# A searched table that assigns small operations to engines, Silu in five front chunks, and newly searched instruction orders, in a Conformer block on one core

## The chip, the cores and the metric

The kernel runs on one core of a Trainium2 chip. Its time is what the device needs for one execution, in microseconds (us). Engines are named as the profiler names them: PE multiplies matrices (PEld loads its weights), ACT evaluates functions, DVE and POOL do element-wise work, SP issues transfers.

## The reference

One Conformer block on x of shape (2, 4000, 144) in bf16, with four heads of width 36:

```python
h = _layernorm(x); x = x + 0.5 * (_silu(h @ w_ff1a) @ w_ff1b)          # 144 -> 576 -> 144
h = _layernorm(x); q, k, v = split heads of h @ w_qkv
p = _softmax(q @ k^T * Dh ** -0.5)                                     # 4000 x 4000, per batch and head
x = x + (p @ v) @ w_o
h = _layernorm(x) @ w_pw1; a, b = halves of h
h = a * _sigmoid(b)
c = depthwise convolution of h over time, 5 taps
x = x + _silu(c) @ w_pw2
h = _layernorm(x); x = x + 0.5 * (_silu(h @ w_ff2a) @ w_ff2b)
return _layernorm(x)
```

The largest part is attention: for each of 2 batches and 4 heads 4000 x 4000 scores, their exponentials, and the sums over values.

## The kernel before

**Tiling.** The 8000 tokens are cut into 16 chunks of 500 (`CH`), eight to a batch; a chunk is four blocks of 125 tokens. For each chunk the kernel runs the first feed-forward, the projections to Q, K and V, attention, the output projection, the gated convolution, and the second feed-forward. Attention of one chunk goes over 62 key tiles of 64 keys (`KT_ROWS`) and a rest of 32. One tile holds the scores of all four heads (PE, four quarter-array matmuls `PS<-QT,KT`), their exponentials (`PT<-PS`) and the sums (`PS<-PT,VA`). There are 1008 tiles in all, written in the constant `TYPES` by a letter each. An "A" tile takes its exponential on ACT, as one instruction over 128 x 1000. A "D" tile takes it on DVE in five instructions (two conversions `PT<-PS` of 128 x 500 to an integer form, two bit operations and one product `PT<-PT` of 128 x 1000); it leaves two factors, so that PE needs eight sum matmuls in place of four. "R" is the rest tile of a chunk.

**How the order comes about.** The Python code first runs a planner. Coroutines (one for each step of each chunk: `ln`, `ff`, `residual`, `proj`, `glu`, `conv`, `epilogue` and so on) ask for an engine and buffers, and a cost model picks which goes next. Every operation is noted with what it reads and writes (`R.op`). The instructions are issued by one helper line, so that all have the same line in the profile (L546 before, L580 after), and tiles tell them apart. The planner's result is then replaced: `settle` builds the attention tiles anew from `TYPES`, `BANKS` and `SLOTS`, and `arrange` sorts each engine's instructions into the order written out in the constant `ORDER`; the waits follow from the dependencies.

```python
lines[e] = [o for i in at for o in blocks[keys[i]]]
```

Here `at` is the decoded string of `ORDER` for engine `e`. So the order on every engine is fixed at build time, and a wait blocks all that stands behind it on that engine.

**Three stages.** In the front only little attention can run: keys and values come chunk by chunk. `silus` counts the front's Silu activations; only when none is left does one table load on ACT change to the exponential's table, and no exponential goes before it. Before the change only chunk 0 uses Silu in the front (six activations); the other chunks take `tanh` on ACT (`TH<-PS`) and form x * (1 + tanh) by one DVE product (`HT<-TH,PS`). In the middle, exponentials run back to back while feed-forwards, projections and convolutions of other chunks fill the other engines. Behind the last exponential lies the tail (`mode["tail"]`): output projection, convolution and second feed-forward of the last chunks, with Silu again.

**Where small operations run.** A LayerNorm (`ln`) is a statistics instruction on DVE (`ST<-X`), one scaling (`RS<-ST`), one power on POOL (`RS<-RS,NHALF`), and one normalisation for each block (`XN`). In the front and tail ("calm") the scaling and the normalisations are DVE's; else POOL's, with one more POOL instruction that negates the mean. Residual additions (`X<-PS,X`) are DVE's. Copies out of PSUM go to DVE, or to ACT where the planner finds it free (`flex`). While PE has nothing to do in the front, the planner puts in products of the identity with itself (`warm`, `PS<-IDENT`).

Of the kernel before, what the change touches and what calls it, by code (L numbers as in the profile page):

```python
# [13 lines left out]
H = 4  # L14
# [21 lines left out]
        '!!!#!$!%!&!(!)!*!+!,!-!.!/!0!1!4!3!5!6!2!7!9!8!;!<!:)^)_)b)c!=!>)k)f)g)j!?!@)n)o!A!B)r)s)v)w!C!D!J!E'  # L36
        '!F!G!H!K!I)a)l!L!P!M!Q!O!N!R!S)y)`)e)t)m)p)q)h)u)d)i)x!U!W!T!V!]!a!`!Y!^!_!c!X!Z!b!g!h!e!i!f!d!j![!l'
        ')z){!n!k*#*!!m*(*&!o!p*+*,*%)})|*)*0*/***3*4*$!q!r*8*7!s*;*<*2*5!t!u!v*?*@*D*-*C*6!w!x*H*G*B*A!y*:*='
        '*K*.*R*Q*9*>*E*L*I*F*V*U!z!{*Y*Z*1*W*_*^*X!|###!!}*b*c*l*m*T*S*]*M*h*i#$#%*y*p*[*q*J*`*a*t*j*u*N#&+!'
        '+#*x*k*o+(+&#(+1+.+-*n*P+7+$*g*f+8+%*r*v*O*w+<+;*d+2+0+/*e+?+@#)+D+C*s+=+9+>+G+H#-#+#*+V+U+J+I+:+K+B'  # L40
        '+++L*z+)*{#,+A+Z*|+*+_+Y+E+,+N+O+F+3*}+5+4+^+6+M+c+b+m+P+l+f+W+X+[+a+q+p#.+t+u+`+g+d+o+x+y#/,$+}+|+w'
        '+]+S+e+n+T,+,,#0,0,/,%+{,!+r+s,3,4#1,8,7+v+R,#,A+k+z,B+j,.+Q,2,-+i,;,E,F,<+h,6,),5,J,I,*,1,9,:,M,N#2'
        ',R,Q,H,?,U,@,G,D,[,]#3,a,`,P,&,V,C,d,e#4,i,h,c,b,(,O,T,l,s,r#5,f,w,v,k,g,j,m,z,{,S#6-#-!,L,W-(,K,X-&'
        '-.--,_,Y,Z,x,u,t-2-1#7,^-6-5,y#8-:-9-3,}-A,>-4,=->-=-8-%,p-7-0,n-B,o-E-F,|-/-K-L-)-<-+-*-;-T-P-O-C-D'
        ',q-S-,-$-Z-@-Y-?-c-b#9#:-^-_-M-]-R-Q#;#<-k-f-g-`-j-J#=#>-o-h-X-n#?#@-I-N-l-H-[-r-q-s-G-x-y#B-}-|-W-e'
        '.%.$#A-d-a.*.)#C-z-i.--{.4.3#D.8.7-v-m-p.<.;#E.?.@.6-U.5...,.+.D.C-w#F.>.H.G.&.:.=.B.A.(.K.L.R.#-V.!'
        '-t.X.Y.J.9#G.^.1.]-u.O.2./.0.F.M.a.b.f.E.S.e.I.N.P.Q.o.p.i#H.s.t.x.w.d#I.r.j.|.{.v._.h.c.V.W.Z/#.[/('
        '/$.y.z.`.q.U/.//#J/2/3.u/).}/&/!/%/6/7/1.m.T.n/:/;#K#L/D/E/8/H/*/I.l.k/0/9/>/=/4/+/M/L#M/?/F/K/P/Q/<'
        '/5/,/T/G#N/N/U/O/X#O/h/i/R/J/Y/_/m/l.g/W/-/b/q/p/`/a#P/{/z/c/@/A/]/S/Z0!0#/C/[/B/V/^0-0.#Q01/t02/k/j'
        '06050&0%/r0$/}/|0(0@0?/n/o0403/u0/0C0D07/s0908000H0G#R0B/f0L0K0:0E0F0A0O0P#S0T0S#T0I0,0_0^0+0R0N0W0M'  # L50
        '0J0b0c0)0*0V0U/g0Q0f0g#U0k0j0X0d0a0e0n0o0i0h0`0>0=0r0s#W#V/w0l0w0v/y/v0z0{0;0m#X0</d1*1)/e/x0y1!0x0]'
        '1-1.#Y12111#1+1,0[0u0t1516#Z191:#[1=1>#]1/101A1B181E171<0}1;0Z1K0p1L0Y1(1F0|1&131O1P0q#^#_1N1S1T1?1I'
        '1X1$1@141W1D1[1J1Q1C1%1b1c#`1g1f1H1M1]1p1q#a1t1u1U1j1i1k1G1y1x1h1s1d1R1e2(2&1r1Y1V2,2+#b201w2*2/1a1v'
        '1|1_1Z2-2:292)1n1}2=2>1z1m#c2.231{1l2B2A1^2<22211o2K2;2L2E2O2P242$2F2?2T2S2%2C2D1`2@2W2X2Q2#2R2g2]2['
        '#d282!26252`2a2U2_#e#f2d2N2m2Y2V2n2M2I2Z272r2h2^2q2J2e2f2c2y2v2u2H2G2b3#3$2z#h3(3)2x2p2o3-3,#g303135'
        '2s2w2l2t34#i3<39383&3+3*3B333C2k3=2i363/3%373G3F#j3J3K2j3.3E3X3U3T3D3I3!3:3N3Y3H2}#k3]3O3?3L3^3@3A2{'
        '3>3h3g3a3;3M323b3Z3l3k3_2|#l3`3o3p3i3}3W3m3n3y3j3R3z3[3V3s3S4!#m4%4&3|3q3Q3e3t41403r3P3f4*4$4#4544#n'
        '49484+4(3{4)4<4=#o#p4@4A474:464;4D4E#q#r4I4H3d3c3x3w3v3u4L4M#s4V4W#t4F4[4Z4G4P#u4`4_4-4X4Y4c4K4J4j4i'
        '4/424Q434,4n4m4>4C4B4?4q4r4.4d#v4v4o4u#w5#5$4p4T4U4O4N4R4b4y5(5)4t4a4z4]4s4x5,5-#x5*51504S4k5+5&5/5.'
        '5;5:4e554f4w4l545%4^5?5>5!4{4}5C5B#y4g5M5@5A4|5L5F4h53525Q5P#z56595D5E5T5U5<5G5N5=585O5Y5X#{5^5]5i5S'  # L60
        '5R5a5b5[5J5K5Z5V575f5e#|5H5W5c5d5_5s5r5I5`5l5h5g5w5v5j5k5{5z5m#}6!5x6#5y6&5}6-6.$!61625t6(5u5|6566$#'
        '$$$%6$6:69645p5n5o6>6=$&6G6H635q6A686%6L6K$(6B6?6<6O6/6P606+6N6)6Y6Z676@6*6M6,6S$)$*6_6^6c6[6R6;6E6]'
        '6I6J6b6T$+6f6F6m6l6q6`6a6d6p6D6C6g$,6t6u6o6Q6x6y$-$.6w6v6}6|7$6e$/7,7+6X6r6U7%7!707#6n6s7/6V6z6k6W79'
        '6{7:73$07=7>7.7-6j7274717A7B$17F7E6i7)7*6h7I7J$2$37M7N7@7Q$47<7C7W7X7G7R7D7[7?7]7H7&7K7L767`7f787;7g'
        '$57a777k7j7(7^757P7_7O7n7o$67x7m7y7r7T7Y7U7Z7p7}7|7V$78$8%7s7z7i7h7S7{8)8*$884838-8#8&7q8(7l8887$98!'
        '7c7b8.8;8<7d86$:8?8@7e7v8C7w8J8I$;8M8N8D8,858+8>8Q8R898L8B8=8K8:8]8[$<$=8`8a8A8P8U7u8^8e8d8V7t8T8O82'
        '$>8l8m8_81808h8c8G8/8i$?8p8g8}8b8Z8y8z8S9!$@8q8r8Y8H8f8o8t8s9%9&8E8X8j8k8n9*9+8W8F9.9495$A99989#9)8{'
        '9$9/9=9<96$B9F9G9@979,8|9-9(9J9K$C9N9O9?9A9H8w8x9R9S9:9I9L9M9V9W$D9b9a8v9Z8u9;9>9f9e9Y$E9[9X9i9j9291'
        '9T9d9P9Q9c9s9t9U9m939x9w9h9E$F9{9n9|9g9B:*909v9D:+9_9`9C:#9u9^:/:.$G:2:$:39]9l:,9z:-9y:0:7:69k:1:::A'
        ':@$H:;9q9r:8:4:9:D:E:H:I:5:B:C:L9}:(:):M:S:R:!9p9o:W:V$I$J:U:J:[:Z:f:e:?:F:>:G:Y:%:&:P:j:_:i:^:]:Q:K'  # L70
        ':`:<:n:m:O:T:h:N:q:=:w:x$K:|:{:r:g:l;$;#$L;.;/:k;!:X:};2;3;7;%:y;&;6:p:z;($M;@;A;::t:a;5:s;E;8;9:b;D'
        ';;;1:o:c;I;H;0:d;4:u;);M;L;C$N$O;J;K:v;F;P;Q;-;B;G;T;U;,$P;X;_;S;`;?;*;>;c;W;d;R;+;<;Y;N;=;V;h;g$Q$R'
        ';k;l;f;e;j;o;i;p$S;s;t;z;m;^;{;];w<%<$<)<*$U$T;y;x<3<4;Z;[;v<-;O<7<8<.;r;u;b;q<<<;;a;n$V<@<?$W$X$[$Y'
        '$Z<C<D<+<=<><G<H<A<:<#<5<9<P<!<2<6<1<L<K<&<B<,<O<(<S$]<Y<Z;|<0<I<T<M<^<_;}</<F<Q<J<i<h$_$^<l<m<]<E<W'
        '<N<b<p<q$`<u<t<j<R<n<c<a<x<y<s<k<r<X<}<|$a$b=+=,<o<z=$<v<w=0=/$c$d=4=3<`=%<[$e$f<{=!=8=7<V=;<f=<=6<U'
        '=1=.<g=#=?=E=F=2=9<d=5=@=J=I$g=M=N=(=G=-=:=)=*=R=Q$h=[=]=H=K=L=&=U<e=a=`$i=d=e=V=^===>=_=C=h=i$j=s=r'
        '=D=l=P=A=O=B=w=v$k={=z=u=S=t=k=j=m>#>!=b=Z=y=x=T=Y>&>($l$m>1>2=c=f>+=g=q=p>5>6$n>:>9=|=}>3=X=W>,>>>='
        '$o>B>A>)>4$p>K>L>7>%><>E>8>;>P>O$q>S>T>$>F>D>*>/>X>W$r$s>->.>]>[>V>C>N>`>M>Z>@>f>g>?>0>U=n=o>Y>k>j>a'
        '$t>i>n>J>I>Q>o>H>l>G>_>s>r$u$v>^>q>e>h>v>w>b>c$w>z$x>y>}?!?%>p?&>t>m>x>u?,?->R>d>{>|?0?1?8?4?5?.?/?>'
        '??$y?C?B?7?9?6?2?3?F?G?@?A?+?J?$?#?Q?P$z?T?U?(?)?D?K?H?I?X?Y?E?*?S?R?=?]?c?d${?h?g?[?Z?^?<?k?l$|?o?p'  # L80
        '$}%!?s?t?:?W@!?m?n?}?;?V?N?b?w@&@%?j?a?L?x?M?e@0@1@+?O?i?r@*@4@5@$@#?`?_?f@<@8@9?q%#@B?v@(@C@=@G@6@.'
        '@7@F@)@3@/@2@-@N@K@J%$@U@,@T@:@I?u@H@Y@X@;%%@O?{@E@^@]@@?|@V@D?z@g@h@[@Z@a@W@l@k%&@s@`@A@L@o@p@??y@j'
        '@S@>@b@y@P@z@R@t@i@M@n@_@}A!%(%)A-A,@Q@{A#@|A0A1%*%+@r@qA;A:%,%-A?A>@d@cA$A3@eABACA4@f%.AFAG@uA=@xA2'
        '@vA<AKAJA5A%AAAD@mAEAOANA.AIA&@wAHA/ASAR%/A@AMAWAV%0%1A[AZA*AQAPA+A`A_%2AcAd%3A8A9AmAn%4ALArAqAYAg%5'
        'AuAvA6AfAXA7AzAyAhAe%6A}B!AoAp%7B*B)B%A]A^B/B0ATAUB#AbB4AaB$B3AwAxB(B&B7B8A(A)B;A|A{AtBBBAAlAkAjAiB<'
        'AsBEBF%8BJB2BIBTB1B6BMB:BSBCBDB5B9BHBXBWBGB-BNBKBcBbBgBLB,BVBfB.BkB[B@B?BZBjBYB>B=B]BuBt%9BxByB|BmBi'
        'B+BeBdB}BQBnBlBRC%C$BzB{BhBoBvBwC/C0%:C3C4BOBUBaB`C#C7C8%;CBCAC2B^C1C*BPC5CECFB_C)C(CJCIC6BrC&C;C:CM'
        'CNBpCDC<CGBsC!CWCXCQBqCCCLC9C[C]CRCP%<CaCOCHC`CeCdC_C^%>%=C-CiC.CYChC@%?CZC?CsClCTCrCvCwC>CSCgCjCfCm'
        'CUCkC=C{Cz%@D)D!D*CyCKCxCVD.C}D-CnC+CuCpD#C|CcC,CbD1D2%AD;D<CoD5CqD,D4D+D?D@D(CtD3D0D&D6DCDD%BDNDMD>'
        'D/DGDQDR%CDUDVDHD=DEDODPDZDYDSD:%DDeDAD%DdD9D$DXDhDiDLDKDJD[D]D^DlDm%EDWDFDpDwDgDvDTDfDzDBDjD{D7DoDq'  # L90
        'DIE#E!%FE(DnE&D_DxDkDuD|DtD8E,E+DyE%%G%HE/E3E)E9E$DcE8DaDbDrD`E*E=E<D}E2E1E0E@EAEHE.DsE-EDEE%I%JEOEN'
        '%K%L%MEREIEGESE:EVE>EWE;EBEFEQE?E6ECEPE7EZEbEaETE[EfEe%NEjEiE4EUEYELEXE5EmEnEMEqEcEdExEw%OE|E{EgEKEk'
        'ErElEoF#F$EpF,EhF)F(%PEyF-F3F2E_E`F!F6EzF%F*F7%Q%RF;F:F5EuF&F4E^F?F>EvE}FBEJF+FIFH%SFMFLF=F@E]FCF<F9'
        'FQFPFA%TF8FYFUFTEsEtFNF`F0F_FSFOFJFKFXF/FcFdFVFWFRF1FlF.FhFgFaFGFbFkFF%UFvFuFoFfFjFeFpFzFyFiFE%VF}G!'
        '%WFnG%F^FZG&FwF{FmF]G+G0G1FtFDFsG4G5G*G(G#G)G8G9G<FxGCGBF[%XG=G6GGGFG$G7GJGKG2G/G:G;%YF|GNGDGUG3GTG@'
        '%ZGYGXGEFqGOGIG^GHG-G]G?GLG.GMFrGaGgGh%[G[GVGZGbG>GlGkG`GWG,GjG_GSGRGuGvGAGoGzGy%]GpH!G}GnGeH&GiG|H%'
        '%^G{H#GQH*H+GfGsGPH/H.%_H9GtH3H2GdH,H(H)GmGrH?H@GqH:H6H1GwHDGcHCH-H4HHH0HOHGGxH8H7H$H5HLHKHYHUHVHPH='
        'H>HZHI%`H_H^HMH;HNHEHcHhHiHWHXHJHbH[HmHlH]HBHtH<HqHpHFHAHuHaH`H{Hz%a%bI!I#%c%d%eI&I(HsHjHrHfHkHgHnI%'
# [2280 lines left out]
```

## Time and profile before

| | |
|---|---|
| median of 3 runs | 885.76 us (885.52 to 889.05) |
| profiled execution | 882.88 us, span 881.0 us |
| first exponential on ACT | starts at 22.50 us |
| attention tiles on ACT / on DVE / rest | 789 / 203 / 16 |
| PE instructions | 11549 matmuls |
| DMA | 26.11 MB, mean 30 GB/s |

The span is the time between the first and the last instruction that the profiler shows. Busy time is the time in which an engine has at least one instruction under way. Consecutive instructions of ACT, DVE and PE overlap a little, so that the mean duration of one is longer than the distance between two. In the chain that ended last every line is a start, a length, an engine and what it worked on, and a chain is followed back from the last instruction to what released it.

### The profile page before, as it was taken

To read this page: it belongs to the slowest core of one execution; us is meant where nothing else is said; L and a number is where in the kernel's file an instruction comes from. 1 tells how busy PE (TensorE), PEld (TensorE's weight loads), DVE (VectorE), ACT (ScalarE), POOL (GpSimd) and SP (SyncE) were. 2 spreads that over 40 slices of the span, in tenths; PEclk is the share of its full clock that TensorE was granted. 3 is DMA by queue.
4 is the path that set the end of the run, shared out by engine and by line. 5 is a ranking of instruction groups with operands and counts; after the bars stand their busy time and mean duration, and the time that the engine had idled before them with its cause. 6 is when DMAs were issued, how large, how long until landed. Compare 5 with 4: busy or idle time off the path is not lost.

```text
span 881.0 us, 26916 instructions
## 1 busy us (share of the span) xinstructions
PE 857.6 (97%) x11549; PEld 412.0 (47%) x11549; DVE 833.1 (95%) x1825; ACT 837.6 (95%) x1074; POOL 281.5 (32%) x544
## 2 busy tenths in 40 slices
PE   7999999999999999999999999999999999999996
PEld 7543434444444444434444444444444434444485
DVE  7999999999999999999999999899999999999888
ACT  4889999999999999999999999999999999999965
POOL 6660341051223402711420141301630541403534
PEclk9999999999999999999999999999999999999999
DMA  4321121112121110321220020110120111101101
GB/s 123 67 33 20 24 41 26 32 26 44 20 38 39 30 10 2 62 26 25 45 26 2 9 37 1 28 18 20 26 44 2 28 39 31 21 6 27 26 17 43
DMA packets 83551, 26.11 MB, mean 30 GB/s; under 512 B 78231, under 2 KB 83432, under 8 KB 83432
## 3 DMA queue, kind: packets, MB, share of 16 engines
q1 hardware_dynamic: 81886, 23.70, 14.9%
q8 instruction: 90, 1.47, 0.7%
q10 hardware_dynamic: 1546, 0.69, 0.3%
q14 instruction: 29, 0.24, 0.1%
HBM read 3.31 MB, written 2.30 MB: 6 GB/s over the span
## 4 chain that ended last, share of the span: by engine, by line
ACT 64%; PE 26%; DVE 6%; DMA 1%; POOL 1%; issue 0%; DVEq 0%
ACT PT L546 59%; PE PS L546 26%; ACT TH L546 5%; DVE HT L546 2%; DVE PT L546 1%; DVE ST L546 1%; DVE X L546 1%; DVE XN L546 1%; DMA XTB<-XN 1%; DMA X<-in_x_dram 0%; DVE KT L546 0%; POOL XN L546 0%; DVE QT L546 0%; POOL RS L546 0%; ACT HT L546 0%
## 5 line engine op out<-in xcount | busy, mean ns | idle before, releaser
L546 ACT ACTIVATE PT<-PS 128x1000 bf16<-128x1000 f32 (+1 forms) x805 | 740.8, 1081 | 8.7 <-PE PS L546 7.6
L546 PE MATMUL PS<-QT,KT 64*64 64x500 bf16 x3968 | 457.8, 385 | 7.2 <-ACT PT L546 3.0
L546 PE MATMUL PS<-PT,VA 64*37 64x500 bf16 x4780 | 448.1, 373 | 1.1 <-DVE QT L546 0.6
L546 DVE TENSOR_SCALAR PT<-PS 128x500 int16<-128x500 f32 x405 | 266.8, 673 | 14.3 <-PE PS L546 11.3
L546 PEld LDWEIGHTS PS<-QT,KT 64*64 64x64 bf16 x3968 | 138.2, 104 | 213.5 <-ACT PT L546 123.1
L546 PEld LDWEIGHTS PS<-PT,VA 64*37 64x37 bf16 x4780 | 163.0, 96 | 106.8 <-issue 17.6
L546 POOL TENSOR_SCALAR RS<-ST 125x4 f32<-125x4 f32 x118 | 34.3, 291 | 506.6 <-DVE ST L546 500.8
L546 DVE TENSOR_SCALAR PT<-PT 128x1000 uint16<-128x1000 uint16 x406 | 164.7, 418 | 2.6 <-PE PS L546 0.7
L546 DVE TENSOR_TENSOR PT<-PT 128x1000 bf16<-128x1000 bf16 x203 | 136.8, 676 | 1.5
L546 POOL TENSOR_SCALAR XN<-X,RS 125x144 bf16<-125x144 bf16 x236 | 128.3, 555 | 6.2
L546 POOL TENSOR_TENSOR RS<-RS,NHALF 125x4 f32<-125x4 f32 (+2 forms) x99 | 95.3, 967 | 46.1 <-DVE RS L546 40.9
L546 ACT ACTIVATE TH<-PS 128x500 bf16<-128x500 f32 (+3 forms) x175 | 95.8, 572 | 5.7 <-PE PS L546 4.9
L546 DVE SCALAR_TENSOR_TENSOR HT<-TH,PS 128x500 bf16<-128x500 bf16 (+1 forms) x120 | 72.2, 617 | 3.9 <-ACT TH L546 3.0
L546 PE MATMUL PS<-XTB,WA 72*128 72x500 bf16 (+2 forms) x304 | 72.2, 347 | 0.4 <-DVE HT L546 0.2
L546 DVE BATCH_NORM_STATS2 ST<-X 125x6 f32<-125x288 bf16 (+1 forms) x160 | 66.1, 448 | 0.7 <-DMA X<-in_x_dram 0.3
L546 DVE SCALAR_TENSOR_TENSOR X<-PS,X 125x288 bf16<-125x288 f32 x128 | 57.1, 452 | 6.7 <-PE PS L546 5.4
L546 PE MATMUL PS<-WB,HT 128*125 128x144 bf16 (+1 forms) x640 | 51.8, 231 | 0.2 <-ACT HT L546 0.2
L546 PEld LDWEIGHTS PS<-WB,HT 128*125 128x125 bf16 (+1 forms) x640 | 45.5, 138 | 11.6 <-issue 5.1
L546 PEld LDWEIGHTS PS<-XTB,WA 72*128 72x128 bf16 x304 | 23.5, 98 | 27.5 <-issue 11.7
L546 ACT ACTIVATE HT<-PS 128x500 bf16<-128x500 f32 (+3 forms) x46 | 21.0, 528 | 7.7 <-PE PS L546 6.8
L546 PE MATMUL PS<-U,DG 128*128 128x375 bf16 (+5 forms) x204 | 27.5, 263 | 0.0
L546 DVE TENSOR_SCALAR XN<-X,ST,RS 125x144 bf16<-125x144 bf16 (+1 forms) x80 | 22.3, 356 | 2.1 <-POOL RS L546 1.8
(89 smaller groups left out, 505.2 us busy)
## 6 DMA issues: line engine op xcount, KB each, us to landing
X<-in_x_dram SPq DMA_DIRECT2D x16, 140.6 KB
XTQ<-XTB SPq DMA_DIRECT2D x24, 70.3 KB
out_dram<-XN SPq DMA_DIRECT2D x11, 140.6 KB
XTB<-XN SPq DMA_TRANSPOSE x50, 3.1
out_dram<-XN SPq DMA_DIRECT2D x7, 70.3 KB
XTB<-AN SPq DMA_TRANSPOSE x15, 4.0
WA<-in_w_ff1a_dram ACTq DMA_DIRECT2D x1, 144.0 KB
WB<-in_w_ff1b_dram ACTq DMA_DIRECT2D x1, 144.0 KB, 2.6
```

The source lines that it names most:

```text
L546: ins = getattr(eng, o.name)(*o.a, **o.k)
```

## The change

- Each small operation that could run on another engine is noted with its alternatives (`R.unit`): a copy out of PSUM on DVE or ACT; LayerNorm's scaling on DVE or POOL; its normalisations on DVE, POOL or ACT; a residual addition on DVE, or on ACT, in which case two more PE products add X, times a scaled identity (`EYE`), into the same PSUM bank; the copy of an attention result on DVE or ACT. The constant `UNITS` holds a letter for each, and `choose` replaces the planner's choice where the letter differs (80 places).
- LayerNorm's normalisation on POOL subtracts the mean itself; the negation is gone.
- `warm` products fill no waits any more: 50 stand at the start, where 111 stood before in all.
- Front chunks 0 to 4 (`NSIL = 5`) use Silu for the first feed-forward. `silus` starts at 26, and no exponential is taken before they are done.
- The first chunk of X is loaded in two halves. The table load for Silu stands ahead of the weight loads on ACT's queue. POOL's clearing writes stand behind the first two powers.
- An A tile may use two PSUM banks that are not neighbours.
- `ORDER`, `PLACES`, `TYPES`, `BANKS`, `SLOTS` and the planner's parameters (`POLICY`, `TJ`) are new; the planner's latency of a transposing transfer goes from 2.0 to 2.6. There are 798 A tiles and 194 D tiles.

The diff, cut to its core:

```diff
+UNITS = (
+    'ddddddadadddaddadaaadaadaddaadddd...
+)
...
+    def choose(self, codes):
+        for code, (ops, own, alts, extras, ends) in zip(codes, self.units):
+            if code == own:
+                continue
+            more = []
+            for eng, name, a, k, cost, kind, tile, deps in extras.get(code, ()):
+                o = Op()
...
+                more.append(o)
+            if any(o.eng == "pe" for o in more):
+                for o in ends:
+                    o.k["stop"] = False
+            for o, (eng, name, a, k, cost, lat) in zip(ops, alts[code]):
+                o.eng, o.name, o.a, o.k = eng, name, a, k
...
+                o.deps = o.deps + [(x, True) for x in more]
+            self.ops += more
...
+    NSIL = 5
+    SILQ = 1
...
-    LAT_T = 2.0
+    LAT_T = 2.6
...
-    load_x("sp", 0)
+    op("pool", "memset", NHALF[:, :], -0.5, w=["NHALF"])
+    for g in range(2):
+        load("sp", f"x0{g}", X[0:TB, 2 * g:2 * g + 2, :], x_tok[0][:, 2 * g:2 * g + 2, :], ...)
+    op("act", "activation", DUM[:, :], NHALF[:, 0:1], ACT.Silu, bias=0.0, scale=1.0, ...)
     load_ff("act", "w0", "w3", WA1, WE1, WB1, w_ff1a, w_ff1b, "W1", 3.5, 4.5)
...
+    op("pool", "tensor_scalar", EYE[:, 0, :], IDENT[:, :], 2.0, None, op0=ALU.mult, r=["ID"], w=["EYE2"], cost=0.4)
+    op("pool", "tensor_scalar", EYE[:, 1, :], IDENT[:, :], 4.0, None, op0=ALU.mult, r=["ID"], w=["EYE4"], cost=0.4)
...
-    R.filler = warm
+    R.filler = None
...
-    silus = [6]
+    silus = [6 + 5 * (NSIL - 1)]
...
+        for j in range(n):
+            a = (xn(u, j), xi(j), ST[0:rows, u, j, 1:2], RS[0:rows, u, 0, j:j + 1])
+            k = dict(op0=ALU.subtract, op1=ALU.mult)
+            alts["d"].append(("dve", "tensor_scalar", a, k, 0.231, None))
+            alts["p"].append(("pool", "tensor_scalar", a, k, XN_COST, XN_LAT))
+            alts["a"].append(("act", "activation", (xn(u, j), xi(j), ACT.Identity),
+                              dict(bias=RS[0:rows, u, 2, j:j + 1], scale=RS[0:rows, u, 0, j:j + 1]), 0.41, None))
...
+        R.unit([o], "d", {"a": [("act", "activation", (xv(c, bs, rows), ps, ACT.Copy), dict(bias=0.0, scale=scale),
+                                 c_act(2 * D), None)]},
+               {"a": [("pe", "matmul", (PSV[0:rows, bk, i * D:(i + 1) * D],), dict(
+                   lhsT=eye[0:rows, 0:rows], rhs=X[0:rows, c * NB + b, :], start=False, stop=True, ...), 0.0645, "f", ends[0].tile, deps)
+                      for i, b in enumerate(bs)]}, ends)
...
-        yield from ff(c, s, WA1, WE1, WB1, "W1", False, None)
+        yield from ff(c, s, WA1, WE1, WB1, "W1", c < NSIL, None)
...
     def settle():
+        R.choose(UNITS)
...
-        if n >= NIT or len(eq) >= now("MAXQ"):
+        if n >= NIT or len(eq) >= now("MAXQ") or silus[0] > SILQ:
...
-        if eq and len(ptp.free) > owed[0] and silu_done:
+        if eq and len(ptp.free) > owed[0] and silus[0] <= 0:
```

## The prediction

> **What bounds the kernel now.** I read the busy shares on the page first, then the table of windows, then the chain that ended last.
>
> ```profile
> span 881.0 us, 26916 instructions
> PE 857.6 (97%) x11549; PEld 412.0 (47%) x11549; DVE 833.1 (95%) x1825; ACT 837.6 (95%) x1074; POOL 281.5 (32%) x544
> ```
>
> Three engines are at 95% or more, so the shares alone decide nothing. The windows are cut at the first exponential on ACT (22.5 us) and behind the last (833.5 us). Columns: stretch, length, busy us (instructions) of PE, weight loads, DVE, ACT and POOL, granted PE clock, DMA share, GB/s.
>
> ```profile
> 0.00:22.50 22.50, 18.02 (x201) 15.68 (x201) 17.56 (x65) 11.19 (x23) 14.79 (x33) 0.92 0.45 123
> 22.50:120.00 97.50, 95.76 (x1324) 47.09 (x1324) 93.96 (x209) 88.91 (x118) 37.33 (x69) 1.00 0.20 35
> 120.00:757.00 637.00, 629.28 (x8564) 281.11 (x8564) 611.38 (x1266) 633.77 (x777) 180.65 (x350) 1.00 0.15 26
> 757.00:773.00 16.00, 14.26 (x177) 5.89 (x172) 13.01 (x27) 13.63 (x18) 9.74 (x21) 0.89 0.28 34
> 22.50:833.50 811.00, 799.55 (x10882) 361.38 (x10882) 775.93 (x1620) 795.83 (x983) 246.61 (x477) 1.00 0.15 27
> 833.50:881.00 47.50, 40.02 (x471) 34.95 (x466) 39.57 (x142) 30.63 (x70) 20.09 (x36) 0.97 0.15 33
> ```
>
> From 120 to 757 us ACT is idle for 3.2 us of 637: it bounds the middle. In front it is busy for 11.2 of 22.5 us, behind the last exponential for 30.6 of 47.5 us; there the chain is another engine's:
>
> ```profile
> 584.00 0.96 ACT TH L546 x2
> 587.99 26.03 ACT PT L546 x29
> ...
> 757.83 1.04 POOL RS L546
> 759.28 3.47 POOL XN L546 x4
> 762.77 4.89 DMA XTB<-XN
> ...
> 829.65 31.55 PE PS L546 x371
> ...
> 876.30 1.22 DVE XN L546 x5
> ```
>
> The reader is to see the rate of a fed ACT, 26.03/29 = 0.898 us an exponential and 0.48 us a 500-wide activation; a hole at 757.8 where a LayerNorm's own transfer came late; and a tail that runs on PE. The groups by form (busy, mean ns):
>
> ```profile
> L546 ACT ACTIVATE PT<-PS 128x1000 bf16<-128x1000 f32 x789 | 734.1, 1089 | 8.7 <-PE PS L546 7.6
> L546 PE MATMUL PS<-PT,VA 64*37 64x500 bf16 x4780 | 448.1, 373 | 1.1 <-DVE QT L546 0.6
> L546 DVE TENSOR_SCALAR PT<-PS 128x500 int16<-128x500 f32 x404 | 265.6, 672 | 14.3 <-PE PS L546 11.3
> L546 DVE TENSOR_SCALAR PT<-PT 128x1000 uint16<-128x1000 uint16 x406 | 164.7, 418 | 2.6 <-PE PS L546 0.7
> L546 DVE TENSOR_TENSOR PT<-PT 128x1000 bf16<-128x1000 bf16 x203 | 136.8, 676 | 1.5
> L546 DVE SCALAR_TENSOR_TENSOR X<-PS,X 125x288 bf16<-125x288 f32 x126 | 56.2, 452 | 6.7 <-PE PS L546 5.4
> L546 DVE SCALAR_TENSOR_TENSOR HT<-TH,PS 128x500 bf16<-128x500 bf16 x96 | 63.1, 669 | 3.1 <-ACT TH L546 2.2
> L546 DVE TENSOR_SCALAR XN<-X,ST,RS 125x144 bf16<-125x144 bf16 x78 | 21.8, 357 | 2.1 <-POOL RS L546 1.8 <-issue 0.2
> L546 ACT ACTIVATE HT<-PS 128x250 bf16<-128x250 f32 x13 | 5.0, 384 | 0.1
> ```
>
> An exponential keeps ACT busy for 734.1/789 = 0.930 us on average, against 0.898 in the fed run: (0.930 - 0.898) x 789 = 25 us of late starts that the busy time hides. With the 15.2 us of plain idle in the middle some 40 us there can be won without taking any work away.
>
> **Work that moves between engines.** Counts are from the two programs' instruction orders. Nine attention tiles go from DVE to ACT (exponentials 789 to 798, DVE tiles 203 to 194). A DVE tile is 2 x 0.657 + 2 x 0.406 + 0.674 = 2.8 us, so DVE loses 25 us; ten residual additions (0.446 each), 16 normalisations (0.28) and four tanh products (0.657) take off 11.6 more, and 15 more small statistics operations give some 2 back. A DVE tile needs eight sum matmuls where an ACT tile needs four: 36 fewer at 448.1/4780 = 0.094 us, -3.4 us on PE, of which the 20 new matmuls that add X through a (scaled) identity take back under 2. Neither PE nor DVE bounds the middle, so these count only through what they let ACT do.
>
> ACT by stage, at 0.48 us for 500 columns, 0.3 for 250 and for the 288-wide residual (an estimate, between half of 0.48 and the 0.385 of the isolated 250-wide row), 0.45 for a normalisation and 0.2 to 0.3 for the small ones, with these rows for the normalisation (the fifth) and, further below, the start and the last chunk's store:
>
> ```profile
> 0.74 0.66 ACTq L546 DMA_DIRECT2D WA<-in_w_ff1a_dram  x1
> 4.04 1.28 ACT L546 ACT_TABLE_LOAD   x1 [4.04 <-issue]
> 10.51 1.82 ACT L546 ACTIVATE HT<-PS 128x500 bf16<-128x500 f32 x4 [2.10 <-PE PS L546]
> 22.50 1.90 ACT L546 ACTIVATE PT<-PS 128x1000 bf16<-128x1000 f32 x2
> 861.19 0.90 ACT L546 ACTIVATE XN<-X,RS 125x144 bf16<-125x144 bf16 x2
> 866.29 0.24 ACTq L546 DMA_DIRECT2D out_dram<-XN  x1
> ```
>
> Before the first exponential: 16 wide and 4 half Silu, two transposed copies, one value copy, two residuals, two normalisations more, three tanh and one copy fewer: 7.7 + 1.2 + 1.0 + 0.5 + 0.6 + 0.9 - 1.4 - 0.5 = +10.0 us. Between first and last: nine exponentials 8.1, four normalisations 1.8, four residuals 1.2, two projections 1.0, tanh 0.9, two copies -1.0: +12.0 us. Behind the last: 12 wide and five half Silu, four copies, three convolution pairs and four normalisations fewer, four residuals and two tanh more: -11.4 us. ACT has 10.6 us more to do in all. That is the heart of the case: the engine that bounds the middle gets more work.
>
> **The front.** Exponentials now wait until the 26 Silu of five chunks are through (one switch of tables behind them, as before behind six). The first then starts behind 11.2 + 10.0 = 21.2 us of ACT work plus ACT's idle time, now 11.3 us. Two things can add to it. First, POOL's series of clearing writes goes from before the first statistics to behind them:
>
> ```profile
> 1.45 0.58 POOL L546 MEMSET WP2Z<- 128x576 bf16 x1
> 3.45 0.52 POOL L546 MEMSET WK<- 128x512 bf16 x1
> 7.36 1.85 POOL L546 MEMSET AN<- 128x1024 bf16 x2
> ...
> 6.78 2.52 DVE L546 TENSOR_SCALAR XN<-X,ST,RS 125x144 bf16<-125x144 bf16 x4 [0.84 <-POOL RS L546]
> 11.85 0.54 DVE L546 TENSOR_SCALAR XN<-X,ST,RS 125x144 bf16<-125x144 bf16 x2
> ```
>
> Four normalisations took 2.52 us beside two clearing writes of 1.85 us, where two alone take 0.54: DVE stood still until they were done. The Trainium skill (SBUF — State Buffer, Who interferes with whom) says why: a DVE tensor_scalar in a two-port mode and a GpSimd instruction lock each other out for the whole instruction. By that rule, and the trace agrees, the new series of one AN write and the 2.5 us from WP2Z to WK (0.9 + 2.5 = 3.4 us) holds the second half's normalisation 1.6 us longer than the 1.85 us of now. Against it stands the first chunk's X, loaded as two halves, and a conversion (IDF) that no longer stands in the same lock: between nothing and 1.6, I take 0.8 us. The feed-forward weights, issued at 0.74 us now, come behind the table load of 1.28 us on ACT's queue, some 1.5 us later; they lie beside the normalisation, whose end at 9.3 us (6.78 + 2.52) is what the first feed-forward waits for. First exponential: 21.2 + 11.3 + 0.8 = 33.3 us.
>
> **The middle.** Busy time 795.8 + 12.0 = 807.8 us. What comes back: the 97.5 us behind the first exponential, where ACT was idle 8.6 us beside a DVE 96% busy, lose sixteen DVE products (10.5 us) to the Silu; the hole at 757 us (2.4 us idle) belongs to one transfer in one order, and the new order is built on a longer transposition latency. I let idle time fall from 15.2 to 9 and a third of the 25 us of late starts go, 8.4: DVE, whose late release holds PE's banks, has 4% less to do. 807.8 + 9 - 8.4 = 808.4 us.
>
> **The tail.** The second feed-forward of three chunks moves ahead of the last exponential. PE instructions behind the last sum fall from 464 to 315, DVE's from 143 to 96, ACT's from 69 to 43. DVE at 39.57/142 = 0.279 us each loses 13.1 us, PE at 40.02/471 = 0.085 loses 12.7; the tail is bound by those two, the last chunk's own chain being shared in both. Less whichever stays, 12.9 to 13.3: 47.5 - 13.3 = 34.2 us. The chain of the last chunk alone (it stored from 866 us, 33 us behind the last exponential, while sharing PE with six others) bounds it below, by my estimate at 30 us.
>
> **The sum.** 33.3 + 808.4 + 34.2 = 875.9 us of span against 881.0, that is -5.1. The profiled execution took 882.88 us, 1.9 more than its span; the median of the three runs is 885.76. The difference on the median gives 880.5 us (-0.6%). Half a percent, 4.4 us, is about what a measurement of this kernel can tell from no change.
>
> **The rivals.** *ACT's load decides (slower).* If neither idle time nor late starts shrink, the middle is 807.8 + 15.2 = 823.0 and the sum 33.3 + 823.0 + 34.2 = 890.5: +9.5, or 895 us. For it: 3.2 us of idle in 637 show an ACT with nothing to gain from a lighter DVE, and the orders are new and may bring holes of their own like the one at 757. Against: the 25 us of late starts. It decides as soon as less than 9.5 us of the 40 come back.
>
> *PE's clock in front (no change).* 61 of the 111 identity products between the first steps go.
>
> ```profile
> 6.00:8.00 2.00, 0.58 (x7) 1.00 0.26 78
> 8.00:10.00 2.00, 0.65 (x11) 1.00 0.34 121
> 12.00:13.00 1.00, 1.00 (x8) 0.50 0.67 175
> 13.00:14.00 1.00, 1.00 (x11) 0.50 0.60 148
> ```
>
> (Stretch, PE busy, granted clock, DMA.) After 4 us with PE busy a third of the time the clock falls to 0.50 for the work from 11 to 14.5 us. Without products in the waits of 14 to 21 us there can be such a stretch again, and some 3 us more of matmuls at half clock put the first exponential at 36.3 us: 883.5 on the median. The Trainium skill (TensorE: Matmul & The Clock Gate, Part 1: The HAM clock gate) tells the same: the array's clock halves when it has been idle and needs some 3.4 us of activity to return; by that rule the filler pays. For it: the rows. Against: the new order puts the next chunks' feed-forward there.
>
> *Everything closes up (much faster).* First exponential at 31, two thirds of the late starts gone, tail 31: 31 + 800 + 31 = 862, or 867 us.
>
> **How the numbers follow.** The forecast 0.35 and the much faster case 0.10; no change, by the clock or by a gain that stops halfway, 0.27; ACT's load 0.28. So faster 0.45, same 0.27, slower 0.28. The range goes from just above the fast case, 868, to just short of the full slower one, 894.
>
> **What would show it.** First exponential near 33 us; ACT idle between first and last exponential near 9 us and 798 exponentials at about 0.92 us busy each; 34 us behind the last. An exponential at 0.93, or idle of 15 us and more, means the slower rival; a granted clock under 0.9 in the first 35 us the second; a tail over 40 us would show the last chunk's chain, not its load, to be the bound.

## The result and the profile after

The changed kernel takes 913.97 us (median of 4 runs, 910.68 to 916.42); the kernel before took 885.64 us in the runs beside it. The ratio is 1.0333, with an interval from 1.0302 to 1.0365: slower by 3.3%, where the prediction had 0.6% faster and its range ended at 894 us. The profiled execution took 916.42 us with a span of 914.2.

The page of the changed kernel, busy time by engine:

```profile
span 914.2 us, 26582 instructions
PE 870.2 (95%) x11440; PEld 405.3 (44%) x11440; DVE 810.1 (89%) x1768; ACT 848.5 (93%) x1091; POOL 369.9 (40%) x478
```

ACT is busy for 10.9 us more than before (848.5 against 837.6), as forecast (10.6). PE is busy for 12.6 us more (870.2 against 857.6) with fewer instructions, at a lower granted clock, as the windows below show. What stands out is POOL: it has 66 instructions fewer than before (478 against 544) and is busy for 88 us more (369.9 against 281.5). The windows, cut at the first exponential (40.65 us) and behind the last (880.35 us), columns as in the prediction:

```profile
0.00:40.65 40.65, 31.98 (x292) 24.31 (x292) 24.52 (x91) 21.94 (x47) 24.04 (x47) 0.88 0.43 89
40.65:880.35 839.70, 811.59 (x10831) 358.02 (x10831) 759.08 (x1591) 807.87 (x1003) 321.37 (x397) 0.98 0.14 26
880.35:914.20 33.85, 26.65 (x325) 22.96 (x317) 26.54 (x88) 18.66 (x44) 24.46 (x34) 0.96 0.13 34
```

The tail is as forecast (33.85 against 34.2 us). ACT's busy time in the middle is 807.87 us; the prediction had added up 807.8. But the middle is 839.7 us long: ACT is idle for 31.8 us in it, not 9. The first exponential comes at 40.65 us, not 33.3. So the span is 38.3 us above the forecast's 875.9: 7.35 in front, 31.3 in the middle, -0.35 in the tail.

Groups by form (busy us, mean ns | idle before): POOL's normalisation before, the same as changed, the exponential as changed. Then waits (engine, what waits, for what: us in total, times, longest), two from before and three as changed:

```profile
L546 POOL TENSOR_SCALAR XN<-X,RS 125x144 bf16<-125x144 bf16 x236 | 128.3, 555 | 6.2
L580 POOL TENSOR_SCALAR XN<-X,ST,RS 125x144 bf16<-125x144 bf16 x250 | 246.3, 996 | 5.6 <-PE PS L580 1.8
L580 ACT ACTIVATE PT<-PS 128x1000 bf16<-128x1000 f32 x798 | 746.3, 1084 | 21.3 <-PE PS L580 20.0
```

```profile
ACT PT L546 <- PE PS L546: 7.6, 16, 1.4
PEld PS L546 <- DMA XTB<-XN: 3.1, 3, 2.1
ACT PT L580 <- PE PS L580: 20.6, 30, 4.4
PEld PS L580 <- DMA XTB<-XN: 17.8, 9, 4.5
PE PS L580 <- DMA XTB<-XN: 14.3, 7, 4.3
```

POOL's normalisation takes 0.996 us where the old form took 0.555. PE waits for transpositions of normalised data, and ACT waits for PE: a chain of three. The chain that ended last shows it at one place of the middle:

```profile
346.27 1.03 POOL RS L580
347.30 7.26 POOL XN L580 x8
...
354.96 1.34 POOL RS L580
...
356.83 7.16 POOL XN L580 x8
364.00 3.31 DMA XTB<-XN
367.33 2.53 DMA XTQ<-XTB
369.87 1.04 issue
370.91 1.51 PE PS L580 x5
```

Two pairs of LayerNorms stand in POOL's queue, 7.26 and 7.16 us of normalisations; their transposition lands at 367.3, a second transfer behind it at 369.9, PE starts at 370.9, and ACT starts again at 372.5 us after 4.45 us of waiting. Waits of this kind also cost clock: in the trace the granted clock falls to 0.50 four times in the middle, for 6.8 us each (the first at 153.5, the second at 372 us), and not once in the middle of e1_add below, where POOL is quick again.

In front, the transposition that the fifth Silu chunk needs is issued behind the last loads of X and lands 8.65 us later (first the chain, then SP's queue):

```profile
21.76 8.65 DMA XTB<-XN
...
30.46 26.09 PE PS L580 x257
```

```profile
17.01 4.71 SPq L580 DMA_DIRECT2D X<-in_x_dram  x8
21.76 4.86 SPq L580 DMA_TRANSPOSE XTB<-XN  x1
```

And then PE runs at half clock (stretch, its length, busy us and instructions of PE, PEld, DVE, ACT and POOL, granted clock, DMA share, GB/s):

```profile
26.00:28.00 2.00, 0.13 (x3) 0.00 (x0) 0.98 (x4) 0.66 (x2) 0.88 (x2) 1.00 0.45 123
28.00:30.00 2.00, 0.00 (x0) 0.00 (x0) 0.00 (x0) 0.00 (x0) 0.00 (x0) 1.00 0.57 98
30.00:32.00 2.00, 1.54 (x4) 0.56 (x5) 0.00 (x0) 0.58 (x1) 0.00 (x0) 0.65 0.00 0
32.00:34.00 2.00, 2.00 (x7) 0.90 (x6) 0.50 (x2) 1.18 (x3) 0.00 (x0) 0.50 0.00 0
...
40.00:42.00 2.00, 2.00 (x37) 1.16 (x38) 1.08 (x5) 1.35 (x2) 1.34 (x3) 0.79 0.02 8
```

PE has nothing to do for 4.3 us, and behind that it works for 10.2 us at 0.50 (twice the clock that the windows from 30 to 42 us lack).

### The profile page after: what moved, and what is told of

Its sections match the earlier page's. It is cut to its first block, busy times and chain, and to the rows that moved or that the text cites. A ratio compares the mean times of both kernels' runs of the same rounds, so it can differ in the third digit from the quotient of the medians.

```text
span 914.2 us, 26582 instructions
## 1 busy us (share of the span) xinstructions
PE 870.2 (95%) x11440; PEld 405.3 (44%) x11440; DVE 810.1 (89%) x1768; ACT 848.5 (93%) x1091; POOL 369.9 (40%) x478
## 4 chain that ended last, share of the span: by engine, by line
PE 37%; ACT 35%; DVE 11%; POOL 10%; DMA 6%; issue 1%; SPq 0%; POOLq 0%; DVEq 0%
PE PS L580 37%; ACT PT L580 31%; POOL XN L580 7%; DVE PT L580 6%; DMA XTB<-XN 4%; ACT TH L580 3%; POOL RS L580 2%; DVE ST L580 2%; DVE X L580 1%; DMA XTQ<-XTB 1%; DVE HT L580 1%; DMA XTB<-AN 1%; DVE QT L580 0%; DMA X<-in_x_dram 0%; DVE XN L580 0%
## 5 line engine op out<-in xcount | busy, mean ns | idle before, releaser
L580 ACT ACTIVATE PT<-PS 128x1000 bf16<-128x1000 f32 (+1 forms) x814 | 752.9, 1076 | 21.8 <-PE PS L580 20.6
L580 DVE TENSOR_SCALAR PT<-PS 128x500 int16<-128x500 f32 x387 | 256.4, 674 | 26.7 <-PE PS L580 23.4
L580 POOL TENSOR_SCALAR XN<-X,ST,RS 125x144 bf16<-125x144 bf16 x250 | 246.3, 996 | 5.6 <-PE PS L580 1.8
L580 DVE TENSOR_SCALAR PT<-PT 128x1000 uint16<-128x1000 uint16 x388 | 159.9, 424 | 3.5 <-PE PS L580 1.7
L580 DVE TENSOR_TENSOR PT<-PT 128x1000 bf16<-128x1000 bf16 x194 | 131.0, 677 | 1.7
L580 POOL TENSOR_SCALAR RS<-ST 125x4 f32<-125x4 f32 (+1 forms) x40 | 9.6, 241 | 219.3 <-DVE ST L580 219.3
L580 PE MATMUL PS<-XTB,WA 72*128 72x500 bf16 (+2 forms) x288 | 75.8, 369 | 13.8 <-DMA XTB<-XN 13.6
L580 DVE SCALAR_TENSOR_TENSOR HT<-TH,PS 128x500 bf16<-128x500 bf16 (+1 forms) x115 | 70.0, 617 | 19.8 <-ACT TH L580 18.7
L580 DVE BATCH_NORM_STATS2 ST<-X 125x6 f32<-125x288 bf16 x160 | 66.2, 450 | 4.9 <-POOL XN L580 2.2
L580 DVE SCALAR_TENSOR_TENSOR X<-PS,X 125x288 bf16<-125x288 f32 (+1 forms) x118 | 52.5, 451 | 15.5 <-PE PS L580 14.7
L580 POOL COPY U<-U 128x2 bf16<-128x2 bf16 (+1 forms) x54 | 11.2, 243 | 60.7 <-DVE U L580 43.5
L580 DVE CAST KT<-PS 128x500 bf16<-128x500 f32 (+1 forms) x29 | 19.2, 665 | 12.5 <-PE PS L580 12.2
```

The lines of the kernel that those rows point to most:

```text
L580: ins = getattr(eng, o.name)(*o.a, **o.k)
```

## The experiments

The theory after the result: POOL's normalisation in its new form costs nearly twice as much and makes the LayerNorms late in the middle; in front a late transposition and the half clock add the rest. Rivals: the new orders themselves bring the holes; something else slows POOL; the feed-forward work of five chunks decides the front.

The pieces of the span, each from the windows of the kernel's profiled execution:

| kernel | to the first exponential | to the end of the last | tail | span |
|---|---|---|---|---|
| before | 22.50 | 811.00 | 47.50 | 881.0 |
| forecast | 33.3 | 808.4 | 34.2 | 875.9 |
| changed | 40.65 | 839.70 | 33.85 | 914.2 |
| e1_add | 37.60 | 813.13 | 33.57 | 884.3 |
| e2_before_sub | 20.94 | 836.22 | 49.34 | 906.5 |
| e4_late_x | 39.04 | 841.83 | 33.93 | 914.8 |
| e5_both | 40.48 | 813.58 | 33.64 | 887.7 |
| e6_all | 31.32 | 813.41 | 33.57 | 878.3 |
| e7_before_noid | 26.59 | 812.16 | 47.55 | 886.3 |
| e8_add_prod | 38.52 | 813.02 | 33.56 | 885.1 |
| e10_all_again | 33.11 | 814.62 | 33.57 | 881.3 |
| e11_before_fill | 20.86 | 808.08 | 49.16 | 878.1 |

The first column scatters from execution to execution, and each row is one execution: e10_all_again is the same kernel as e6_all and comes 1.8 us later, and e2_before_sub, whose front is that of the kernel before, comes 1.6 us earlier than before.

### e1_add: the old form back

```diff
-            alts["p"].append(("pool", "tensor_scalar", a, k, XN_COST, XN_LAT))
+            z = ((xn(u, j), xi(j), RS[0:rows, u, 2, j:j + 1], RS[0:rows, u, 0, j:j + 1]) , dict(op0=ALU.add, op1=ALU.mult))
+            alts["p"].append(("pool", "tensor_scalar", *z, XN_COST, XN_LAT))
...
-        R.unit(ops, code, alts, {"a": [("dve", "scalar_tensor_tensor", (), dict(
+        R.unit(ops, code, alts, {"p": [("pool", "tensor_scalar", (RS[0:rows, u, 2, 0:n], ST[0:rows, u, 0:n, 1], -1.0, None),
+                                       dict(op0=ALU.mult), 0.24, None, None, ())], "a": [("dve", "scalar_tensor_tensor", (), dict(
...
```

The last lines of the excerpt put the negation of the means on POOL ahead of the normalisations.

> The changed kernel with POOL's normalisation in the form of before: a negation of the means, then add and multiply with both scalars from RS; every order and every choice of engine as changed. Theory (the form): a POOL normalisation falls from 0.996 us to 0.46 to 0.56 us, a LayerNorm of four on POOL from some 4 us to 2.2 with its negation, two queued ones from 8 to 4.5; ACT's idle time between the first and the last exponential falls from 31.8 us to about 10 and the time to 886 to 893 us. Rival (the new orders): the normalisation falls as well, but the holes come from the new sequence on PE and ACT: idle stays over 25 us, time over 905. Rival (contention on POOL): the normalisation stays near 1 us in the old form, since it is other traffic that slows it, and the time stays at 912 to 918.

Measured: 886.83 us, ratio to before 1.0058 (1.0034 to 1.0082). The group, the middle window and the waits:

```profile
L581 POOL TENSOR_SCALAR XN<-X,RS 125x144 bf16<-125x144 bf16 x250 | 136.2, 559 | 7.6 <-POOL RS L581 2.3 <-PE PS L581 0.2
```

```profile
37.60:850.73 813.13, 800.96 (x10831) 354.26 (x10831) 758.84 (x1592) 804.59 (x1003) 236.57 (x457) 1.00 0.15 27
```

```profile
ACT PT L581 <- PE PS L581: 6.6, 14, 1.1
PEld PS L581 <- DMA XTB<-XN: 1.2, 2, 0.7
```

With one operation exchanged and a negation more for each LayerNorm, in the same orders, the middle is 26.6 us shorter, ACT's idle time in it 8.5 us, its granted clock 1.00 instead of 0.98, and PE hardly waits for a transposition. The form is the cause of the loss in the middle; the new orders as such bring no holes. The same place of the chain as above, where each pair now takes some 4.5 us:

```profile
337.26 2.50 POOL XN L581 x4
340.05 1.80 POOL XN L581 x4
...
344.78 2.29 POOL XN L581 x4
347.44 1.81 POOL XN L581 x4
349.26 3.05 DMA XTB<-XN
```

### e2_before_sub: the new form in the kernel before

```diff
-    op("pool", "tensor_scalar", xn(u, j), xi(j), RS[0:rows, u, 2, j:j + 1],
-       RS[0:rows, u, 0, j:j + 1], op0=ALU.add, op1=ALU.mult,
...
+    op("pool", "tensor_scalar", xn(u, j), xi(j), ST[0:rows, u, j, 1:2],
+       RS[0:rows, u, 0, j:j + 1], op0=ALU.subtract, op1=ALU.mult,
...
```

> The kernel before with only POOL's normalisation in the new form (subtract and multiply, the mean from ST; the negation is still made and not used). Theory (the form): 0.85 to 1.0 us for each of the 236 instead of 0.555, and holes in the middle as in the changed kernel: 895 to 915 us. Rival (contention in the new order): the rows stay at 0.46 to 0.56 and the time at 884 to 887.

Measured: 907.27 us, ratio 1.0285 (1.0233 to 1.0337).

```profile
L546 POOL TENSOR_SCALAR XN<-X,ST,RS 125x144 bf16<-125x144 bf16 x236 | 231.7, 992 | 6.2
```

The same 0.99 us and nearly the same loss (25.2 us more in the middle) in orders that have nothing else of the change.

### e3_add_st and e9_mult_sub: which half of the form costs

```diff
-            alts["p"].append(("pool", "tensor_scalar", a, k, XN_COST, XN_LAT))
+            alts["p"].append(("pool", "tensor_scalar", a, dict(op0=ALU.add, op1=ALU.mult), XN_COST, XN_LAT))
...
```

> The changed kernel with add in place of subtract in POOL's normalisation, the mean still read from ST, no negation (this adds the mean where the reference subtracts it). It tells the two halves of the form apart. If the operation costs: rows of 0.46 to 0.56 us and 882 to 890 us. If the operand in ST costs: rows of 0.85 to 1.0 us and 912 to 918 us.

```diff
-                op("pool", "tensor_scalar", xn(u, j), xi(j), RS[0:rows, u, 2, j:j + 1],
-                   RS[0:rows, u, 0, j:j + 1], op0=ALU.add, op1=ALU.mult,
+                op("pool", "tensor_scalar", xn(u, j), xi(j), RS[0:rows, u, 0, j:j + 1],
+                   RS[0:rows, u, 2, j:j + 1], op0=ALU.mult, op1=ALU.subtract,
...
```

> The kernel before with POOL's normalisation as multiply first and subtract second, both scalars in RS (this computes another value: the mean is not scaled). If subtract costs in any place: about 0.86 us in the median instead of 0.46, and 900 to 912 us. If it costs only as the first operation: 0.46 us in the median and 880 to 886 us.

Measured, one execution each: 890.22 us with add (a hair above its range, with the first exponential at 40.40 us, but a middle of 813.95 us as in e1_add), 911.21 us with subtract in the second place. The view of the tile `XN` gives count and least/median/longest ns; in this order the changed kernel, e3_add_st, before, e9_mult_sub:

```profile
L580 POOL TENSOR_SCALAR XN<-X,ST,RS x250: 838/856/2266, 20.2 to 907.9; 125x144 bf16<-125x144 bf16 x125
```

```profile
L580 POOL TENSOR_SCALAR XN<-X,ST,RS x250: 452/460/1896, 20.1 to 880.9; 125x144 bf16<-125x144 bf16 x125
```

```profile
L546 POOL TENSOR_SCALAR XN<-X,RS x236: 453/461/1648, 23.3 to 835.3; 125x144 bf16<-125x144 bf16 x118
```

```profile
L546 POOL TENSOR_SCALAR XN<-X,RS x236: 837/851/2840, 25.3 to 862.4; 125x144 bf16<-125x144 bf16 x118
```

Where the mean comes from makes no difference; the operation does. A subtract on POOL, in either place, takes 0.85 us in the median for 125 x 144, an add 0.46. The least time moves with it (838 against 452 ns), so it isn't other traffic that slows POOL.

### e4_late_x: the front's loads behind the transposition

```diff
 lines[e] = [o for i in at for o in blocks[keys[i]]]
+late = [o for o in lines["sp"] if o.q in [f"x{c}" for c in range(8, 16)]]
+rest = [o for o in lines["sp"] if o not in late]
+i = [i for i, o in enumerate(rest) if o.name == "dma_start_transpose"][0] + 1
+lines["sp"] = rest[:i] + late + rest[i:]
```

> The changed kernel with the loads of the last eight chunks' X issued behind the first transposition by DMA instead of ahead of it. Theory (a transfer decides the front): the transposition that is issued at 21.8 us and lands at 30.4 lands near 25 to 26; ACT's 4.75 us of waiting in front and the half clock behind it go, the first exponential comes at 34 to 36 us instead of 40.65, time 4 to 6 us less (908 to 911). Rival (the feed-forward matmuls of five chunks decide the front): the first exponential stays above 39 us, time within 2 us of the changed kernel.

Measured: 914.50 us, ratio 1.0326 (1.0275 to 1.0377), no different from the changed kernel. The first exponential came at 39.04 us. In this execution two normalisations of the first chunk on DVE took 3.44 us instead of 1.48, until POOL's clearing writes (5.92 to 9.34 us) were done; so the first Silu started at 10.40 us instead of 8.85, the clock fell twice, and the transposition was issued only at 28.1 us because its own LayerNorm was late. Alone, the edit shows nothing; the theory missed, and by its marks the rival held. That the feed-forward work doesn't hold the first exponential at 39 us is shown by e6_all below (31.32 us with all of that work).

### e5_both, e8_add_prod and e6_all: the front taken apart

e5_both has the edits of e1_add and e4_late_x. e8_add_prod and e6_all add 46 identity products to e1_add and to e5_both (`again` copies one of the 50 at the start):

```diff
+if e == "pe":
+    for i, n in [(102, 28), (54, 18)]:
+        more = [self.again(lines[e][1]) for _ in range(n)]
+        lines[e][i:i] = more
+        self.ops += more
```

> The changed kernel with add on POOL again (as e1_add) and the last eight chunks' X loaded behind the first transposition (as e4_late_x), no products added. If the transposition's landing costs something beside the clock: ACT's longest wait in front shrinks and the first exponential comes 1 to 3 us before e1_add's 37.6 us, time 884 to 887. If the granted clock decides the front: a stretch of 0.5 lasts 10 us or more again, the first exponential stays at 36 to 40 us, and the time within 2 us of e1_add's 886.8.

> As e1_add with the 46 identity products of e6_all, the X loads where the change has them. If the clock alone decides: time within 2 us of e6_all. If the transposition behind the loads costs as well: PE waits for it for 3 to 5 us at 26 us, the clock falls there as in the changed kernel, and the time is 3 to 8 us above e6_all.

> As e5_both, and 46 identity products in PE's two waits in front: 18 between the transposes of the first chunk's halves and 28 behind the residual products of the first feed-forward. Theory (the clock in front): no stretch of 0.5, or one under 4 us; the first exponential at 30 to 34 us, the time 877 to 882, faster than the kernel before. Rival (the products change nothing, the front is bound by ACT's or PE's own work): the first exponential at 36 to 39 us and the time as e5_both.

Measured, ratio to before: e5_both 885.11 us, 1.0037 (1.0008 to 1.0066); e8_add_prod 888.08 us, 1.0093 (1.0060 to 1.0127); e6_all 880.50 us, 0.9984 (0.9967 to 1.0001). The loads alone bring nothing sure (e1_add had 1.0058), the products alone nothing; both together bring 4.6 us on e5_both and 7.6 on e8_add_prod. In e8_add_prod the products fill the wait at 12 us, but PE still waits for the transposition behind the loads, and the half clock comes after that; first its row of the chain, then windows:

```profile
21.35 8.35 DMA XTB<-XN
```

```profile
28.00:30.00 2.00, 0.25 (x2) 0.14 (x3) 0.00 (x0) 0.00 (x0) 0.00 (x0) 1.00 0.36 70
32.00:34.00 2.00, 2.00 (x8) 0.99 (x7) 1.78 (x8) 1.09 (x3) 0.22 (x1) 0.50 0.00 0
```

In e6_all both waits are gone and the granted clock is 1.00 up to the first exponential. The transposition, with no loads ahead of it, takes 1.35 us in SP's queue instead of 4.86, and PE doesn't wait for it; first its row, then windows:

```profile
21.27 1.35 SPq L598 DMA_TRANSPOSE XTB<-XN  x1
```

```profile
0.00:31.32 31.32, 29.31 (x338) 24.09 (x338) 23.93 (x90) 21.37 (x46) 21.95 (x48) 1.00 0.38 106
31.32:844.73 813.41, 800.93 (x10831) 354.30 (x10831) 758.67 (x1592) 804.66 (x1003) 235.56 (x457) 1.00 0.16 27
844.73:878.30 33.57, 26.63 (x325) 22.98 (x317) 26.24 (x88) 18.64 (x44) 20.31 (x39) 0.98 0.13 35
```

e5_both, without products, scatters from 879.47 to 889.95 us; the mean granted clock of those two executions was 0.998 and 0.990. Its profiled execution (889.84 us, clock 0.988) is one of the long ones. Its time fits both of its expectations and decides nothing between them. What the loads' place is worth depends on whether the clock falls elsewhere: two of its ten executions kept a mean clock of 0.998 without any product and took 879.47 and 880.25 us, while with the products all ten of e6_all had 0.997 or more. So, by these times, the products bring no more than a clock that holds by itself; they make sure of it.

### e7_before_noid and e11_before_fill: the products in the kernel before

```diff
+        idle = {id(o) for o in self.warm[50:]}
+        lines["pe"] = [o for o in lines["pe"] if id(o) not in idle]
...
```

```diff
+                for i, n in [(57, 22), (50, 20)]:
+                    more = [self.again(lines[e][1]) for _ in range(n)]
+                    lines[e][i:i] = more
...
```

The first excerpt is of e7_before_noid, the second of e11_before_fill.

> The kernel before without the 61 identity products that it issues between the first steps (the 50 at the start stay); orders and choices as before. Theory (the clock in front): a longer stretch at 0.5 than the 4 us of before, the first exponential 2 to 8 us later than 22.5 us, the time 885 to 891. Rival (in this order of the front the work itself keeps the clock): first exponential within 1 us, the time 881 to 885.

> The kernel before with 42 more identity products, 20 at the end of those at the start and 22 between the first chunk's halves. Theory (the clock in front): its 4 us at half clock from 10.5 us go, the first exponential comes 1 to 3 us before 22.5, the time is 880 to 882. Rival (ACT's chain decides there): first exponential within 0.5 us, time within 1 us of before.

Measured: 888.29 us, ratio 1.0079 (1.0054 to 1.0104), without; 879.27 us, ratio 0.9958 (0.9941 to 0.9975), with 42 more. The windows up to the first exponential, without, then with more:

```profile
0.00:26.59 26.59, 20.30 (x144) 15.20 (x144) 18.55 (x65) 12.09 (x23) 17.07 (x38) 0.73 0.43 122
```

```profile
0.00:20.86 20.86, 19.01 (x243) 16.93 (x243) 17.56 (x65) 11.09 (x24) 14.80 (x33) 1.00 0.46 126
```

ACT's work in front is much the same (12.09 and 11.09 us); the first exponential moves from 26.59 over 22.50 to 20.86 us with the clock (0.73, 0.92, 1.00). The products of before were worth 5.3 us there by the spans and the medians (7 by the ratio), and 42 more are worth another 0.4%. This is the one version that is surely faster than the kernel before, and it has nothing of the change in it.

How it gains is told better by all executions than by one pair of profiles. Of the 2.9 us between the two spans 1.6 are in front; the middle is 2.9 us shorter too, because the hole at 757 us, which the prediction put down to the order, isn't there in the same order (ACT is busy for 15.95 of the 16 us from 757 us), and the tail is 1.7 us longer. Of the 23 executions of the kernel before that stood beside it, six had a mean granted clock of 0.998 or more and took 879.46 to 880.45 us; the other 17 had 0.990 to 0.996 and took 882.31 to 886.77. All eleven with more products had 0.996 or more and took 878.67 to 880.49. The products bring every execution to where one in four came by itself.

### e10_all_again: a narrower interval

> The kernel of e6_all once more, for a narrower interval against the kernel before: 879 to 882 us, a ratio of 0.995 to 0.999.

Measured: 882.01 us, ratio 0.9994 (0.9973 to 1.0015): both just outside what was expected. With both its faults mended the change makes no difference that can be measured: the tail is 13.9 us shorter, the front 8.8 longer, the middle 2.4 longer (e6_all against before, by the table), and of the 2.7 us that this leaves the two ratios show 0.5 to 1.4, the medians 2.1 to 2.5.

## Why the prediction was wrong

**The step that failed** is a term that the sum doesn't have: the normalisation of the LayerNorm on POOL, whose form changes in the diff, was put at nothing without a reason. I saw only the negation that went (0.29 us of POOL for each of some 60 LayerNorms), and the prediction doesn't mention the exchange of add for subtract. The row to ask was there: before, `XN<-X,RS` on POOL at 0.555 us was always an add, and no POOL subtract stood in the trace, so the new form was an operation that the trace did not show and should have been bounded. It costs 0.44 us more (0.996 against 0.559 with the same orders), four times for each LayerNorm, less the 0.277 us of the negation: 1.5 us of latency, 3 where two are queued. That is what brought idle time of ACT in the middle to 31.8 us. The exchange back is worth 26.6 us of the 31.3 us missed there (e1_add), and 25.2 us are lost in the other kernel by the same edit (e2_before_sub).

**The first exponential** was forecast at 33.3 us: 21.2 of ACT work, 11.3 idle, 0.8 for POOL's clearing writes. ACT's work was 21.94 us; its idle time 18.7. The rival "PE's clock in front" named the mechanism and sized it too low, at 3 us: a chain of the late transposition and 10 us at half clock. Mended, the first exponential comes at 31.3 us in e6_all and at 33.1 in e10_all_again, that is at the forecast or before it. The 0.8 us for the lock was the middle of two cases, and the runs show both. In the changed kernel's own execution (and in e1_add, e3_add_st, e6_all and e8_add_prod) the second half's two normalisations took 1.48 us, and the first Silu started at 8.76 to 8.85 us where before it started at 10.51. In e4_late_x, e5_both and e10_all_again, with the same orders on DVE and POOL, they took 3.44 us, which is the 3.4 us of the working, and the first Silu started at 10.40 to 10.55. So the term is right in kind, and 0 or 1.6 to 1.8 us in an execution; what decides which isn't shown. I gave the transposition no part in the front at all, though the change adds chunks to the Silu phase whose normalised data go through a transposition by DMA.

**The middle.** Apart from the holes the term for ACT's load held: 807.87 us busy as changed, 804.6 in e1_add, e5_both, e6_all and e8_add_prod, where 807.8 was forecast; idle 8.5 us in e1_add and 8.75 in e6_all where 9 was. What failed here too are the 8.4 us of late starts that were to come back and bring ACT's busy time to 799.4. An exponential kept ACT busy for 0.935 us on average in the changed kernel (746.3/798) and 0.938 in e6_all (748.4/798), not 0.92, and the middle of the mended kernels is 813 to 815 us, not 808.4. DVE's load fell by less than the terms add up to: 23.0 us in all (833.1 to 810.1), where 25 and 11.6 less 2 were forecast. And a DVE that is busy for 17 us less in the middle (758.8 against 775.9) didn't make an exponential any shorter.

**The tail** was right: 34.2 forecast, 33.85 as changed, 33.6 in the mended kernels. The 13.3 us taken off is a little more than either of its two terms (13.1 for DVE, 12.7 for PE), so that the last 0.4 us of the agreement are luck.

**The rival "ACT's load decides"** had the sign, but not the mechanism: its 823.0 us of middle never came, because the idle time did fall once POOL was as quick as before. It had said that the new orders may bring holes of their own; the holes came, but from the form of one instruction and not from the orders.

## What to carry to other kernels

When an edit exchanges one operation for another on the same engine, price it even if it looks free; here a one-line form change in an instruction that runs 250 times and stands in a chain of latencies outweighed all the rest of a searched order. An order searched with a cost model that has one price for both forms (`XN_COST` is 0.5 in both kernels) is searched for another machine, so put the measured price of each form in first. Filler on PE in front is judged by the granted clock of the windows behind each wait, and here a filled wait was worth nothing while another one further on remained. Where one kernel scatters by 7 us with its granted clock, compare many executions and their clocks before a difference of 2 us is put down to an edit.

## What the runs showed of the hardware that I had not expected

POOL's `tensor_scalar` on 125 x 144 in bf16 takes 0.46 us in the median with add and multiply, and 0.85 to 0.86 us as soon as one of the two operations is a subtract, first or second, whichever tile the scalar stands in (four kernels, 236 to 250 instructions each). The Trainium skill (GPSIMD Engine Reference, 3.1 Elementwise — side-by-side cycle accounting) gives a price of an element-wise operation in cycles for an element; here the operation alone makes a factor of 1.86.

Once the granted clock has fallen, it stays at 0.50 for long under full work. In e1_add PE was busy for 0.40 of the 2 us from 12 us, and then for all of each 2 us up to 28 us at half clock:

```profile
12.00:14.00 2.00, 0.40 (x7) 0.25 (x4) 1.93 (x10) 0.98 (x3) 1.78 (x4) 1.00 0.55 145
14.00:16.00 2.00, 1.94 (x15) 1.49 (x16) 1.90 (x9) 1.44 (x3) 2.00 (x4) 0.62 0.56 160
...
26.00:28.00 2.00, 2.00 (x17) 1.82 (x16) 1.28 (x4) 0.57 (x2) 0.01 (x1) 0.50 1.33 160
28.00:30.00 2.00, 2.00 (x13) 1.04 (x12) 1.09 (x4) 1.47 (x3) 2.00 (x3) 0.97 0.44 86
```

That is 13.6 us (twice the clock that the windows lack, times their length). The Trainium skill (TensorE: Matmul & The Clock Gate, Part 1: The HAM clock gate) gives some 3.4 us of sustained work for the way back. The stretches in front here, worked out so from windows of 1 us, were 3.4 us (before), 6.8 (e2_before_sub, e8_add_prod), 10.2 (changed, e3_add_st, e9_mult_sub) and 13.6 (e1_add), and two each in e4_late_x (3.4 and 10.2), e5_both (6.8 and 10.2) and e7_before_noid (6.8 and 17.1): one to five times 3.41 us, and nothing between. So the clock came back only in steps of 3.41 us, and a wait cost up to five of them, although the profile has PE busy in nearly all of that time. Nor does every wait bring it: the same wait from 12 to 14 us in the changed kernel left the clock at 1.00. What decides between the two is not settled by these runs.
